# Two chunks per scan, scaled q and k in place, and a state gain every second chunk, in a fused HGRN2 and feed-forward kernel

## The chip, the cores and the metric

The kernel runs on one core of one Trainium2 chip. The metric is device time in microseconds (us). Three runs of the kernel before gave 463.27, 461.01 and 459.28 us, so the median is 461.01 us. One further execution was profiled; its times are in the section on the profile.

## The reference

An attention-like recurrence (4 batches, 8 heads, 768 steps, head width 48) feeds a feed-forward block on 3072 tokens. All data are fp32 on the chip.

```python
f = 1.0 / (1.0 + np.exp(-f_logit))
for t in range(S):
    state = f[:, :, t, :, None] * state + np.einsum('bhd,bhe->bhde', k[:, :, t], v[:, :, t])
    y[:, :, t] = np.einsum('bhd,bhde->bhe', q[:, :, t], state)
x = np.ascontiguousarray(attn_out.transpose(0, 2, 1, 3)).reshape(B * S, H * D)
a = x @ w1                      # w1, w2: 384 x 1024
b = x @ w2
h = a * b @ w3                  # w3: 1024 x 1024
return (h @ w_out)              # w_out: 1024 x 384
```

## The kernel before, in words

**Attention.** The 4 x 768 steps are 24 chunks of 128 steps (`C = 128`, `NU = 24`, six chunks per batch). A chunk's tile has the 8 heads as 2 groups of 48 partitions (padded to 112) and 4 heads of 128 steps side by side, so 512 columns (`NQ`). For each chunk `u`, `front(u)` plans: three pairs of loads (f, k, q, 96 KB each) and one of v; the sigmoid on ScalarE (`gates`, L521); a running product forward over the chunk (`forward`, a scan on VectorE, L529, into tile `fwd`); a copy of its last column (L534); the reciprocal of the last column into tile `back` (`ends`, L539); q times the product (`scale_q`, L545); a running product backward that starts from that reciprocal (`backward`, a scan, L551, into tile `bwd`); k times that (`scale_k`, L559). The scan's other operand (`floor` or `back`) starts the product anew at each head. With q and k scaled so, the chunk's own attention is a masked product of the two.

TensorE then turns k (`turn`, L598, 4 transposes; ScalarE copies the result into `kt`, L731). Every chunk from 4 on is handled by a **visit** (in `rest`), 13 rows of TensorE instructions that are always issued as one block: half of `values(u)` (L658), all of `pairs(u + 1)` (L584, the products of scaled q and k of the next chunk), the other half of `values(u)`, `from_state(u)` (L677), `update(u + 1)` (L690). After it ScalarE copies the outcome out of PSUM (`outcome`, L849, tile `ys`) and copies the products of the next chunk (tile `A`, L707); GpSimd masks them in two halves (`affine_select`, L713); VectorE forms the state in the middle and at the end of the next chunk (`middle`, L763 and L766). The state is carried on with a factor per row: GpSimd multiplies the last product with the next chunk's first gate (`gains`, L813, tile `G`), VectorE multiplies the state by it (L822). The next visit needs the mask, the middle state, the next chunk's q, k and `kt`, and the outcome copied. The outcome goes to DRAM and comes back turned (L870, then the gather `xt<-yt`, L873).

**Feed-forward.** Six blocks of 512 tokens. Weights come in as 8-byte words and are rounded by ScalarE (L1407) and VectorE (L1422, L1426, L1432); w3 and w_out are multiplied into one matrix (`fold`, L1471). Block 0 is plain products (`part`, L902 with 128x256), blocks 1 and half of 2 use seven products for eight (`seven`, L998), the others a larger scheme (`many`, L1153, its sums of weights on VectorE). The last product of each block is `down` (L902 with 128x192). Four PSUM banks (`f0` to `f3`) serve all these products and the transposes; four more (`l4` to `l7`) come free after the last visit.

**What sets the order.** Nothing is issued in program order: `Plan` holds every piece of work with its engine, a cost written in the code, what it depends on, which buffers it takes and a priority, and lists them by the earliest start and then by priority. Each engine's instructions are then issued in that order; the SyncE queue (SP) issues all DMAs in its order. Where the plan leaves TensorE idle early on, products of the constant tile `floor` are issued as filler, one for each 0.43 us:

```python
        if t["eng"] == "PE" and t["at"] < FULL:
            n = int((t["at"] - ready_at) / 0.43)
            if ready_at and n:
                idle(n)
            ready_at = t["end"]
```

Of the kernel before, what the change touches and what calls it, by code (L numbers as in the profile page):

```python
# [36 lines left out]
F32 = mybir.dt.float32  # L37
# [22 lines left out]
NQ = HP * C  # L60
NPE = 2
# [36 lines left out]
NFRONT = 12  # L98
# [28 lines left out]
FLOOR = 2.0**-60  # L127
RANGE = 2.0**-40
# [167 lines left out]
def ranged(ctx, tc, q, k, f_logit, v, w1, w2, w3, w_out, out, ident, w12, wc, left):  # L296
# [21 lines left out]
    gates_ = [keep.tile([P, NQ + 1], F32, name=f"gate{i}") for i in range(2)]  # L318
    inputs = [[keep.tile([P, NQ], F32, name=f"{nm}{i}") for i in range(n)] for nm, n in (("q", 3), ("k", 2), ("f", 2))]
    gate = [t[0:R] for t in gates_]  # L320
    qs, ks, fs = ([t[0:R] for t in ts] for ts in inputs)
# [7 lines left out]
    lasts = keep.tile([R, NU, HP], F32, name="lasts")  # L329
# [23 lines left out]
    early = abp.tile([P, KH, TB], F32, name="ab")[0:R]  # L353
    ks += [early[:, 0], early[:, 1]]
    fs += [early[:, 2], early[:, 3]]
    qs.append(at(12288, NQ)[0:R])
    dns = {nm: at(12288 + DH * i, DH) for i, nm in enumerate(("m1", "u2", "u3"))}

    homes = [lambda t=t: t[:, 0:NQ] for t in [floors] + gates_ + inputs[0] + inputs[1] + inputs[2]]
    homes += [lambda p=p, nm=nm: p.tile([P, NQ], F32, name=nm) for p, nm, n in ((one, "fwd", 1), (one, "bwd", 1), (work, "K", 2), (work3, "Q", 3), (work3, "ys", 3)) for _ in range(n)]  # L360
# [16 lines left out]
    plan.pools["t"][0:4] = [aside] * 4  # L377
    moving = plan.add("PE", 0.0, lambda: None, takes=["ab"], prio=-1e9)
    coming = plan.add("PE", 0.0, lambda: None, takes=["ab"], prio=-1e9)
# [29 lines left out]
    def setup():  # L409
# [3 lines left out]
        for i in range(2):  # L413
            if i == 0:
                nc.gpsimd.memset(ks[i][32:64], 0.0)
                nc.gpsimd.memset(qs[i][32:64], 0.0)
                make_identity(nc, ident)
            else:
                nc.gpsimd.memset(fs[i][32:64], 30.0)
        nc.gpsimd.memset(early[32:64, 2:4], 30.0)  # L420
        nc.gpsimd.memset(early[32:64, 0:2], 0.0)
        nc.gpsimd.memset(qs[2][32:64], 0.0)
        nc.gpsimd.memset(qs[3][32:64], 0.0)
        nc.vector.memset(floor, FLOOR)
        nc.vector.memset(heads(floor)[:, :, 0], 1.0)
        nc.vector.memset(back, 0.0)
        for t in gate:
            nc.vector.memset(t[:, NQ : NQ + 1], 0.0)
        nc.vector.memset(ks[1][32:64], 0.0)
        nc.vector.memset(qs[1][32:64], 0.0)  # L430
        for t in sb:
            nc.vector.memset(t, 0.0)

# [46 lines left out]
    def front(u):  # L480
# [3 lines left out]
        ask = n0 - 30 if u in (0, 1) or u > 3 else turn_of(str(u))  # L484
        ask = [ask, ask + 0.5, ask + 1.0, n0 - (28.2, 28.2, 28.2, 28.2, 12)[min(u, 4)] if u in (0, 1) or u > 3 else ask + VLATE[u - 2] if u in (2, 3) else ask + 1.2]

        def load(dst, src):
            def emit():
                if dst is fs[0] and u == 0:

                    nc.sync.dma_start(dst[0:64], src[u].rearrange("two d n -> (two d) n")[0:64])
# [6 lines left out]
        fu, qu, ku = (x[u if u < 4 else u % n] for x, n in ((fs, 2), (qs, 3), (ks, 2)))  # L498

        def free(n, *names):  # L500

            if u < 4:
                return []
            return asked[8:9] + [tk[u - n if u - n >= 4 else u % n][nm] for nm in names]

# [1513 lines left out]
```

## Time and profile before

| what | value |
|---|---|
| median of 3 runs | 461.01 us (459.28 to 463.27) |
| the profiled execution, whole time | 458.04 us |
| its span, first to last instruction | 456.2 us |
| TensorE busy in the span | 448.7 us, 98% |
| VectorE busy | 371.1 us, 81% |
| ScalarE, GpSimd busy | 212.0 us (46%), 69.1 us (15%) |
| granted TensorE clock | 1.00 |

The whole time is 1.8 us longer than the span. PE is TensorE's matmul, PEld its weight load, DVE VectorE, ACT ScalarE, POOL GpSimd, SP the queue that issues DMAs. In a timeline row the first number is the start in us from the start of the span, the second the duration; a fp32 product gives two records of a matmul.

### The profile page before, as it was taken

How to read it: one execution, taken by the hardware profiler on the slowest of the kernel's cores; microseconds unless marked ns; L12 is line 12 of the kernel's file. 1: busy time of each engine (PE TensorE's matmuls, PEld its weight loads, DVE VectorE, ACT ScalarE, POOL GpSimd, SP SyncE). 2: the span in 40 equal slices, each digit the busy share in tenths (PEclk: the TensorE clock that was granted, in tenths of full speed). 3: DMA queues.
4: the chain of work that ended last, by engine and by line, in shares of the span. 5: the costliest groups of instructions: out<-in, count | busy, mean ns of one | idle time of the engine just before them, and what ended most of it. 6: DMA issues, size and time to landing. Idle time of an engine off the chain costs nothing.

```text
span 456.2 us, 11781 instructions
## 1 busy us (share of the span) xinstructions
PE 448.7 (98%) x4792; PEld 392.5 (86%) x4792; DVE 371.1 (81%) x651; ACT 212.0 (46%) x473; POOL 69.1 (15%) x90
## 2 busy tenths in 40 slices
PE   7999999999999999999999999999999999999996
PEld 6788886666899888889999888899899988889996
DVE  8997899999898999989999699885659466767641
ACT  4565344432234453443323256665665666675300
POOL 9341000131222531223223000000000000000000
PEclk9999999999999999999999999999999999999999
DMA  6897898833236666356323502446365612233111
GB/s 178 268 339 249 300 340 284 271 108 105 71 100 196 180 175 162 105 155 184 97 73 82 147 16 78 138 141 205 132 194 172 204 60 96 91 93 92 37 69 39
DMA packets 43308, 68.74 MB, mean 151 GB/s; under 512 B 5217, under 2 KB 28386, under 8 KB 42226
## 3 DMA queue, kind: packets, MB, share of 16 engines
q1 hardware_dynamic: 43250, 67.95, 48.6%
q8 instruction: 38, 0.62, 0.6%
q14 instruction: 20, 0.16, 0.1%
HBM read 58.88 MB, written 9.04 MB: 149 GB/s over the span
## 4 chain that ended last, share of the span: by engine, by line
PE 95%; DVE 1%; SPq 1%; DMA 1%; POOL 0%; issue 0%; POOLq 0%; DVEq 0%
PE f L902 25%; PE l L1153 15%; PE f L998 13%; PE f L1153 12%; PE f L1471 9%; PE l L902 9%; PE py L658 3%; PE pa L584 2%; PE f L598 2%; PE py L677 2%; PE pa L690 2%; PE f L402 1%; SPq L495 1%; DMA ab<-in_k_dram 1%; DVE K L559 0%
## 5 line engine op out<-in xcount | busy, mean ns | idle before, releaser
L713 POOL TENSOR_SCALAR_AFFINE_SELECT A<-A 64x512 f32<-64x512 f32 (+1 forms) x46 | 46.2, 1004 | 107.8 <-ACT A L707 105.7
L1471 PE MATMUL f<-place 128*128 128x384 f32 x128 | 42.4, 487 | 0.0
L902 PE MATMUL f<-xt,w 128*128 128x256 f32 x192 | 42.1, 380 | 0.0
L902 PEld LDWEIGHTS f<-xt,w 128*128 128x128 f32 x192 | 36.3, 190 | 5.0
L1471 PEld LDWEIGHTS f<-place 128*128 128x128 f32 x128 | 23.9, 190 | 15.5
L902 PE MATMUL f<-place 128*128 128x192 f32 x176 | 31.9, 327 | 0.0
L998 PE MATMUL f<-xt,w 128*128 128x256 f32 x120 | 31.3, 380 | 0.0
L551 DVE TENSOR_TENSOR_SCAN bwd<-gate,back 112x512 f32<-112x512 f32 x24 | 30.4, 1267 | 0.7
L529 DVE TENSOR_TENSOR_SCAN fwd<-gate,floor 112x512 f32<-112x512 f32 x24 | 30.0, 1251 | 1.2 <-ACT gate L521 0.3
L902 PEld LDWEIGHTS f<-place 128*128 128x128 f32 x176 | 28.9, 190 | 0.4 <-issue 0.2
L849 ACT ACTIVATE ys<-py 112x512 f32<-112x512 f32 x22 | 13.1, 597 | 32.4 <-PE py L677 29.9
L1407 ACT ACTIVATE place<-place 128x512 f32<-128x512 uint32 (+2 forms) x24 | 21.4, 890 | 9.7 <-DMA place<-in_w_dram 8.7
L998 PEld LDWEIGHTS f<-xt,w 128*128 128x128 f32 x120 | 22.5, 190 | 2.9
L902 PE MATMUL f<-wc,ab 128*128 128x192 f32 x128 | 23.6, 328 | 0.0
L813 POOL TENSOR_TENSOR G<-lasts,gate 112x4 f32<-112x4 f32 x20 | 12.3, 614 | 72.3 <-ACT lasts L534 28.7
L902 PEld LDWEIGHTS f<-wc,ab 128*128 128x128 f32 x128 | 21.2, 190 | 0.3
L521 ACT ACTIVATE gate<-f 112x512 f32<-112x512 f32 x22 | 13.9, 631 | 16.4 <-DVE bwd L551 7.2
L902 PE MATMUL l<-place 128*128 128x192 f32 x112 | 19.8, 326 | 0.0
L658 PEld LDWEIGHTS py<-A,vt 64*64 64x64 f32 (+1 forms) x672 | 13.3, 127 | 7.3 <-issue 6.3
L998 PE MATMUL f<-place 128*128 128x256 f32 x72 | 19.1, 386 | 0.0
L902 PEld LDWEIGHTS l<-place 128*128 128x128 f32 x112 | 18.5, 190 | 0.1
L658 PE MATMUL py<-A,vt 64*64 64x64 f32 (+1 forms) x672 | 18.0, 223 | 0.2
(288 smaller groups left out, 1063.4 us busy)
## 6 DMA issues: line engine op xcount, KB each, us to landing
place<-in_w_dram SPq DMA_DIRECT2D x21, 512.0 KB, 5.9
A<-in_w_dram SPq DMA_DIRECT2D x19, 512.0 KB, 4.0
place<-in_w_dram SPq DMA_DIRECT2D x8, 1024.0 KB, 6.3
q<-in_q_dram SPq DMA_DIRECT2D x46, 96.0 KB, 2.9
vt<-in_v_dram SPq DMA_DIRECT2D x23, 192.0 KB, 2.9
out_dram<-o SPq DMA_DIRECT2D x23, 192.0 KB, 2.8
k<-in_k_dram SPq DMA_DIRECT2D x44, 96.0 KB, 2.4
yt<-ys SPq DMA_DIRECT2D x44, 96.0 KB, 2.9
```

The costliest lines, as they stand in the source:

```text
L521: nc.scalar.activation(gate[u % 2][:, 0:NQ], fu, AF.Sigmoid)
L529: nc.vector.tensor_tensor_scan(s["P"], gate[u % 2][:, 0:NQ], floor, 0.0, ALU.mult, ALU.max)
L551: nc.vector.tensor_tensor_scan(s["R"][:, ::-1], gate[u % 2][:, NQ:0:-1], back[:, ::-1], 0.0, ALU.mult, ALU.max)
L658: done = nc.tensor.matmul(y_block(u, hp, par, half)[p0 : p0 + w], lhsT=s["v"][half * W : half * W + W, h * D : h * D + w], rhs=s["A"][half ...
L713: nc.gpsimd.affine_select(out=a, in_=a, pattern=pattern, compare_op=ALU.is_ge, fill=0.0, base=0, channel_multiplier=-1,)
L813: nc.gpsimd.tensor_tensor(s["G"], lasts[:, u], heads(gate[(u + 1) % 2][:, 0:NQ])[:, :, 0], ALU.mult)
L849: nc.scalar.activation(ys, py, AF.Copy, accum_out=ysum[:, u : u + 1])
L902: nc.tensor.matmul(out_, lhsT=lhs[i], rhs=rhs[i], start=start and i == 0, stop=i == len(lhs) - 1, skip_group_check=True,)
L998: nc.tensor.matmul(q[nm][:, which * TH : which * TH + TH], lhsT=lhs[i](which), rhs=rhs[i], start=start and which == 0 and i == 0, stop=i = ...
L1153: nc.tensor.matmul(banks[g, c][:, which * TH : which * TH + TH], lhsT=lhs, rhs=x_node(a), start=first and which == 0, stop=True, skip_grou ...
L1407: nc.scalar.activation(part_.bitcast(F32), part_, AF.Copy, bias=2.0, scale=2.0**-51)
L1471: nc.tensor.matmul(w3s["p", jc], lhsT=w3s[jc][:, kc * P : kc * P + P], rhs=wos[:, kc], start=(kc == 0), stop=(kc == KF - 1),)
```

## The change

Chunks 0 to 3 (`ALONE = 4`) keep their own `front`. From chunk 4 on, `front_of_two(e)` serves chunks e and e + 1 together: loads of 192 KB for both, one sigmoid over 1024 columns, one forward scan and one backward scan over 1024 columns with 256 steps for a head, one product each for q and k. The backward scan writes into the gate's tile and the products into the tiles of q and k, so the tiles `fwd`, `bwd`, `K` and `Q` go. The two chunks share one running product, so the even chunk's state needs no gain: `gains` and `state` are planned for the odd chunk alone. A small memset after each backward scan takes the reciprocals out of `back` again, since `back` now serves as the other operand of the forward scan too. The floor of the running product (2^-60) is gone with it, and the limit under which the general path is taken is 2^-80 instead of 2^-40. A visit is planned as two pieces of work, `in` (half the values, then `pairs(u + 1)`) and `v` (the rest): what waits for the pairs, such as the copy of `A` and the mask, now follows `in`.

```diff
+N2 = 2 * NQ
+ALONE = 4
-NFRONT = 12
-FLOOR = 2.0**-60
-RANGE = 2.0**-40
+RANGE = 2.0**-80
...
-    floors = keep.tile([P, NQ], F32, name="floor")
+    floors = keep.tile([P, 2 * C], F32, name="floor")
-    spare = keep.tile([P, NQ], F32, name="back")
+    spare = keep.tile([P, N2], F32, name="back")
+    gates_ = [keep.tile([P, N2 + 2], F32, name=f"gate{i}") for i in range(2)]
+    raw_f = keep.tile([P, N2], F32, name="f")
+    running = keep.tile([P, N2], F32, name="run")
+    inputs = [[keep.tile([P, N2], F32, name=f"{nm}{i}") for i in range(2)] for nm in "qk"]
...
+        nc.vector.memset(floor, SMALL)
+        nc.vector.memset(back[:, 0:NQ], 0.0)
+        nc.vector.memset(heads(back[:, 0:NQ])[:, :, 0], 1.0)
...
+        nc.vector.memset(back[:, NQ:N2], 0.0)
+        nc.vector.memset(back[:, NQ : N2 : 2 * C], 1.0)
...
+    def front_of_two(e):
...
+        def load(dst, src):
+            def emit():
+                for par in range(2):
+                    to = dst[rows(par)].rearrange("p (k n) -> p k n", k=2)
+                    nc.sync.dma_start(to, src[e : e + 2, par].rearrange("k d n -> d k n"))
+            return emit
...
+        one_, two_ = of((e - 4, e - 3), "a", "t"), of((e - 4, e - 3), "v")
+        t["lf"] = moves(2, 394, 300, load(raw_f, f_logit), asked[8:9] + of((e - 2, e - 1), "g"), ask[0], since=since)
+        t["lk"] = moves(2, 394, 300, load(ku, k), asked[8:9] + one_, ask[1], since=since)
+        t["lq"] = moves(2, 394, 300, load(qu, q), asked[8:9] + one_ + two_, ask[2], since=since)
...
+        def gates():
+            nc.scalar.activation(by_run(gate[0:R, 0:N2]), by_head(raw_f), AF.Sigmoid)
+        def forward():
+            nc.vector.tensor_tensor_scan(P_, gate[0:R, 0:N2], back, 0.0, ALU.mult, ALU.max)
+        def scale_q():
+            to = by_head(qu)
+            nc.vector.tensor_tensor(to, to, by_run(P_), ALU.mult)
+        def backward():
+            nc.vector.tensor_tensor_scan(R_[:, ::-1], R_[:, ::-1], back[:, ::-1], 0.0, ALU.mult, ALU.max)
+            nc.vector.memset(heads2(back)[:, :, 2 * C - 1], 0.0)
+        def scale_k():
+            to = by_head(ku)
+            nc.vector.tensor_tensor(to, to, by_run(R_), ALU.mult)
...
-            def visit():
+            def enter():
                 s["py"] = ps.tile([P, 2, NQ], F32, name="py")
                 values(u, 1)
                 if more:
                     pairs(u + 1)
+
+            def visit():
                 values(u, 0)
                 from_state(u)
                 if more:
                     update(u + 1)
-            t["v"] = plan.add(
-                "PE", 0.15 + 0.46 * (2 - 0.5 * opens + 2 * more), visit,
+            t["in"] = plan.add(
+                "PE", 0.15 + 0.46 * (0.5 + more), enter,
                 [t["c"], t["lv"], t["mid"]] + past(u, 1, "y", *([] if opens else ["d"])) + [after[nm] for nm in ("q", "k", "e", "lv") if after],
                 n0 - 998, slack=0.8,
             )
+            t["v"] = plan.add("PE", 0.46 * (1.5 - 0.5 * opens + more), visit, [t["in"]], -1e7)
             if after:
-                after["a"] = after["s"] = t["v"]
+                after["a"], after["s"] = t["in"], t["v"]
...
-        if not closes:
+        if not closes and u >= ALONE and u % 2 == 0:
+            t["d"] = t["mid"]
+        elif not closes:
             def gains():
```

The sums of weights that `many` keeps in dead attention tiles now wait for finer groups of them (`k_old`, `q_old`, `k_new` beside `fronts`).

What the plan makes of it is read from the order of the built kernels. TensorE's matmuls are the same in number and shape, but for the fillers: 24 before, 25 after. A visit's 13 rows still stand together everywhere. Three places matter.

The first is SP's queue around chunk 3's gather (`xt<-yt_585` before, `xt<-yt_575` after), the last one that block 0 waits for. Before:

```order
L870 DMA yt_585<-ys_576 48x4x128 x2
L495 DMA f0_102<-in_f_logit_dram 48x512 x2
L495 DMA k0_100<-in_k_dram 48x512 x2
L495 DMA q1_98<-in_q_dram 48x512 x2
L873 DMA xt_311<-yt_585 128x3x128
L1403 DMA place_111<-in_w_out_dram 128x2x768 x3
L1403 DMA place_111<-in_w3_dram 128x2048
```

After:

```order
L970 DMA yt_575<-ys_566 48x4x128 x2
L588 DMA f_97<-in_f_logit_dram 48x2x512 x2
L588 DMA k0_101<-in_k_dram 48x2x512 x2
L588 DMA q0_99<-in_q_dram 48x2x512 x2
L973 DMA xt_303<-yt_575 128x3x128
L1503 DMA place_110<-in_w_out_dram 128x2x768 x3
L1503 DMA place_110<-in_w3_dram 128x2048
```

The order is the same; the six loads ahead of the gather now bring two chunks and have twice the bytes.

The second is TensorE where the first product of `down` follows the last plain product of block 0. Before (the fillers are L402):

```order
L902 MATMUL f3_1259<-xt_311,w12_59 128x256 x3
L902 MATMUL f0_1271<-xt_311,w12_59 128x256 x3
L902 MATMUL f1_1277<-xt_311,w12_59 128x256 x3
L402 MATMUL f3_1289<-floor_93 128x256 x2
L902 MATMUL f2_1292<-wc_60,ab_522 128x192 x4
L902 MATMUL f3_1299<-place_111 128x192 x4
```

After (the fillers are L412; the rows L768 and L781 end the visit of chunk 7):

```order
L768 MATMUL py_1241<-q1_100,S_1098 48x64 x8
L768 MATMUL py_1241<-q1_100,A_103 48x64 x8
L781 MATMUL pa_201<-vt_1100,kt_1225 48x48 x16
L412 MATMUL f3_1321<-floor_93 128x256 x3
L1002 MATMUL f1_1325<-wc_60,ab_512 128x192 x4
L1002 MATMUL f3_1335<-place_110 128x192 x4
```

The visit of chunk 7 has moved ahead of that place, and three fillers stand there instead of two. One more filler stands alone after the twelfth product of block 0, where none stood, and of two in the start-up one has gone.

The third is ScalarE's order after visits, where `A` is the copy that the mask waits for and `ys` the outcome. Before:

```order
L849 ACTIVATE ys_1547,ysum_108<-py_1468 112x2x2x128
L707 COPY A_104<-pa_203 128x512
L1289 COPY o_1564<-f0_1458 128x192
L521 ACTIVATE gate0_95<-f0_102 112x512
L731 COPY kt_1588<-f2_1574 128x448
L534 COPY lasts_107<-fwd_1602 112x4
```

After:

```order
L798 COPY A_103<-pa_201 128x512
L949 ACTIVATE ys_2258,ysum_107<-py_2183 112x2x2x128
L614 ACTIVATE gate1_96<-f_97 112x1024
L1142 COPY ab_2281<-f0_2129 128x256
L822 COPY kt_2283<-f2_2271 128x448
L798 COPY A_103<-pa_201 128x512
L949 ACTIVATE ys_2353,ysum_107<-py_2285 112x2x2x128
```

The copy of `A` now stands ahead of the outcome of the same visit, and the sigmoid over two chunks can stand between two visits. On TensorE two sets of four transposes now often stand side by side, and from chunk 11 on the visits have less between them: between the visits of chunks 15 and 16 there are four products of 256 columns and eight transposes, between those of 16 and 17 six such products. The first two products of `many` in block 2 now come beside the visits, from chunk 15's on, in bank f3, and the third product of that bank comes only after the last visit.

More of the change, by code (lines that the diff above doesn't have):

```diff
@@ L549, in backward @@
         def backward():
[L550 removed]
+            s["R"] = running[0:R, NQ:N2]
             nc.vector.tensor_tensor_scan(
[L552 removed]
+                s["R"][:, ::-1], gate_of(u)[:, NQ:0:-1], back[:, 0:NQ][:, ::-1], 0.0, ALU.mult, ALU.max
             )
[L555 removed]
+            nc.vector.memset(heads(back[:, 0:NQ])[:, :, C - 1], 0.0)
```

176 lines of the change are left out of this document (108 added, 68 removed).

## The prediction

> **What bounds the kernel now.** I read the page first: busy shares, then the chain of work that ended last.
>
> ```profile
> span 456.2 us, 11781 instructions
> PE 448.7 (98%) x4792; PEld 392.5 (86%) x4792; DVE 371.1 (81%) x651; ACT 212.0 (46%) x473; POOL 69.1 (15%) x90
> PE 95%; DVE 1%; SPq 1%; DMA 1%; POOL 0%; issue 0%; POOLq 0%; DVEq 0%
> ```
>
> TensorE is busy 98% of the span and carries 95% of the chain. An average hides stages, so I cut the span by stage; the columns are the window, its length, busy time and records of PE, PEld, DVE, ACT and POOL, then the granted clock, the DMA share and GB/s. Below them stand the same cuts for the fillers alone (L402: PE, PEld).
>
> ```profile
> 0.00:26.00 26.00, 23.03 (x246) 19.11 (x247) 22.69 (x36) 13.82 (x28) 16.66 (x31) 1.00 0.79 242
> 26.00:60.00 34.00, 33.80 (x332) 29.20 (x331) 29.97 (x35) 16.27 (x33) 5.02 (x5) 1.00 0.86 290
> 60.00:130.00 70.00, 70.00 (x664) 49.67 (x663) 65.70 (x90) 25.03 (x48) 11.18 (x12) 1.00 0.59 185
> 130.00:360.00 230.00, 229.90 (x3075) 209.44 (x3074) 196.11 (x374) 112.07 (x264) 36.22 (x44) 1.00 0.48 139
> 360.00:440.00 80.00, 80.00 (x411) 73.39 (x410) 51.67 (x106) 44.21 (x99) 0.00 (x0) 1.00 0.27 86
> ```
>
> ```profile
> 0.00:26.00 26.00, 10.73 (x38) 8.29 (x39) 1.00 0.79 242
> 26.00:60.00 34.00, 1.93 (x8) 1.04 (x6) 1.00 0.86 290
> 60.00:130.00 70.00, 1.03 (x4) 0.76 (x4) 1.00 0.59 185
> ```
>
> From 26 us on TensorE has no hole to speak of: 33.80 of 34, 70 of 70, 229.90 of 230, 80 of 80, all at clock 1.00. Fillers hide some waits: 1.93 + 1.03 = 2.96 us of them stand behind 26 us. So all that any relief of another engine could win after 26 us is 2.96 + 0.20 + 0.10 = 3.3 us. Before 26 us there are 10.73 us of fillers and 26.00 - 23.03 = 2.97 us of idle TensorE, and there VectorE (22.69 of 26) and the loads (0.79) set the pace.
>
> **The change, part by part.** All sums are against the profiled execution: span 456.2, whole time 458.04. The median of the runs, 461.01, is 2.97 above it; I add that at the end.
>
> *VectorE's relief.* Groups of VectorE, with busy time, mean ns of one, and idle before:
>
> ```profile
> L529 DVE TENSOR_TENSOR_SCAN fwd<-gate,floor 112x512 f32<-112x512 f32 x24 | 30.0, 1251 | 1.2 <-ACT gate L521 0.3
> L551 DVE TENSOR_TENSOR_SCAN bwd<-gate,back 112x512 f32<-112x512 f32 x24 | 30.4, 1267 | 0.7
> L559 DVE TENSOR_TENSOR K<-k,bwd 112x512 f32<-112x512 f32 x22 | 16.9, 770 | 0.4
> L545 DVE TENSOR_TENSOR Q<-q,fwd 112x512 f32<-112x512 f32 x23 | 16.2, 704 | 0.0
> 113.45 0.68 DVE L1504 TENSOR_TENSOR place<-w 128x512 f32<-128x512 f32 x1
> 118.57 0.95 DVE L1518 TENSOR_TENSOR place<-wc 128x768 f32<-128x768 f32 x1
> ```
>
> No row shows 1024 columns. 256 more columns of a plain product cost 0.95 - 0.68 = 0.27, so 512 more cost 0.54 and a product of 1024 takes 0.68 + 0.54 = 1.22. A scan of 1024 lies between 1.25 + 0.54 = 1.79 and 2 x 1.25 = 2.50. I take 2.36: the product's part that does not grow is 0.68 - 0.54 = 0.14, and a scan that saves just that gives 2.50 - 0.14. Per pair of chunks before: 4 x 1.26 + 2 x (0.770 + 0.704) = 7.99; after: 2 x 2.36 + 2 x 1.22 + 0.07 for the memset (my guess from 0.06 for the smallest one below) = 7.23. Ten pairs save some 8 us of VectorE, with a little more for reciprocals and gains left out. None of it reaches the end: the 3.3 us above is the cap, whatever VectorE saves. The same goes for ScalarE (46%), GpSimd (15%) and the fewer loads. Were this cover gone, VectorE's 8 us would be the most to lose or win.
>
> The single `f` tile makes the next pair's load wait for this pair's sigmoid. Two visits, some 10 us, lie between two such sigmoids and a load lands in about 3 us (the next fence but one): nothing. The backward scan now overwrites the gate, so it waits for GpSimd's gain of the chunk before; the forward scan ahead of it (2.36) covers that unless both masks stand in front. Behind it on VectorE are k's product and the middle states, which a visit waits for; I put this wait into the term on visits.
>
> *Start-up.* Here VectorE does bind. In these rows the first figure is the start, the second the duration:
>
> ```profile
> 1.07 0.48 DVE L424 MEMSET floor<- 112x512 f32 x1 [1.07 <-PEq L2006]
> 1.62 0.06 DVE L425 MEMSET floor<- 112x4 f32 x1
> 4.73 1.23 DVE L529 TENSOR_TENSOR_SCAN fwd<-gate,floor 112x512 f32<-112x512 f32 x1 [0.26 <-ACT gate L521]
> 23.92 0.96 DVE L1422 TENSOR_SCALAR place<-place 128x1536 uint32<-128x1536 uint32 x1 [0.30 <-DMA place<-in_w_dram]
> 28.02 1.76 DVE L1432 CUSTOM_DVE_ANT_0 w<-place,w 128x3072 uint16<-128x3072 uint16 x1
> 30.11 4.05 PE L902 MATMUL f<-xt,w 128*128 128x256 f32 x18
> ```
>
> The memsets ahead of the first scan change by: half of `floor` less (-0.24), the second half of `back` more (+0.48), two more gate columns and one more row of ones (3 x 0.06), so +0.42. The scan waited 0.26 for the gate, so it starts 0.16 later. Four memsets behind the backward scans of chunks 0 to 3 add 4 x 0.07 = 0.28. Of these 0.44, the wait of 0.30 for a load at 23.92 swallows up to 0.30. What is left goes through the weights' rounding (28.02) to the first block-0 product at 30.11: **+0.2**, between 0 and 0.5.
>
> *Chunk 3's gather.* Six loads ahead of it have twice the bytes now.
>
> ```profile
> 35.47 32.64 PE L902 MATMUL f<-xt,w 128*128 128x256 f32 x150
> 36.00:48.00 12.00, 12.00 (x57) 10.57 (x56) 9.64 (x10) 5.13 (x12) 1.20 (x1) 1.00 0.80 259
> 42.39 0.39 SPq L873 DMA_DIRECT2D xt<-yt  x1
> DMA to landing us min/median/max: 2.7/3.4/4.1
> ```
>
> The gather is issued at 42.39 and lands within 2.7 to 4.1 us (tile xt), by 46.5 at the latest. A record of these products takes 32.64 / 150 = 0.2176. By the order nine products of six records go ahead of the first that needs chunk 3: 35.47 + 54 x 0.2176 = 47.2, so 0.7 is spare. 576 KB more at 259 GB/s take 2.2 us, which would make the gather 1.5 late if all of it goes first; with the DMA share at 0.80, part finds room. A filler of 0.43 stands there now, so the cost is at least that unless TensorE comes late anyway. I take **+0.45**, between 0.43 and 1.5; 3.0 if the issues double in time as well.
>
> *Three fillers ahead of `down`.*
>
> ```profile
> 123.12 1.03 PE L402 MATMUL f<-floor 112*128 112x256 f32 x4
> 123.39 0.42 DVE L944 TENSOR_TENSOR ab<-f,ab 128x256 f32<-128x256 f32 x1 [0.83 <-PE f L902]
> ```
>
> Two fillers ran 1.03 while VectorE formed `ab` until 123.81: the wait that they cover was real, about 0.7 us. After, a visit's products stand ahead of three fillers; if the wait is gone, the third is pure loss. **+0.45**, one filler; from -0.3 (they start that much sooner on the free engine) to 1.5, where VectorE comes to `ab` a scan late.
>
> *Visits closer together.* One visit before, with the copies, masks and scans behind it:
>
> ```profile
> 152.94 0.45 PE L658 MATMUL py<-A,vt 64*64 64x64 f32 x16
> 153.21 0.64 PE L584 MATMUL pa<-Q,K 48*64 48x64 f32 x32
> 154.62 0.60 ACT L849 ACTIVATE ys<-py 112x512 f32<-112x512 f32 x1 [0.61 <-PE py L677]
> 154.82 1.99 PE L998 MATMUL f<-place 128*128 128x256 f32 x8
> 155.20 0.58 ACT L707 COPY A<-pa 128x512 f32<-128x512 f32 x1
> 155.64 1.23 DVE L529 TENSOR_TENSOR_SCAN fwd<-gate,floor 112x512 f32<-112x512 f32 x1
> 155.85 3.06 POOL L713 TENSOR_SCALAR_AFFINE_SELECT A<-A 64x512 f32<-64x512 f32 x2 [2.57 <-ACT A L707]
> 156.65 0.55 PE L598 MATMUL f<-ident,K 112*128 112x112 f32 x4
> 157.24 1.23 DVE L551 TENSOR_TENSOR_SCAN bwd<-gate,back 112x512 f32<-112x512 f32 x1
> 159.73 0.45 PE L658 MATMUL py<-A,vt 64*64 64x64 f32 x16
> 169.18 1.37 POOL L713 TENSOR_SCALAR_AFFINE_SELECT A<-A 64x512 f32<-64x512 f32 x2 [3.20 <-ACT A L707]
> ```
>
> The visit took 154.82 - 152.94 = 1.88; the next came 6.79 after its start. The masks ended at 158.91, 5.97 after the start, so 0.82 was spare. After, `A` is copied ahead of `ys`. The pairs end at 153.85, so the copy can start about 1.27 sooner, near 153.93: the masks would end 4.70 after the start if they are slow (3.06), 3.0 if they are quick (1.37, as at 169.18). Against that the distance shrinks. By the order shown, chunk 16's visit follows chunk 15's after four products (two records each, 4 x 0.435) and eight transposes (two times 0.55 at most, by the row at 156.65): 1.88 + 1.74 + 1.1 = 4.7 at most. The next comes after six products: 1.88 + 2.61 = 4.5. I count ten visits from chunk 11 on with about 4.5 to 5.5. Quick masks leave 1.4 spare, slow ones nothing, and the sigmoid over two chunks (about twice 0.6) can stand ahead of a copy of `A`. I take **+1.0**, a tenth of a us for each of the ten; from 0 to the 7 us of the first rival.
>
> **Sum.** 0.2 + 0.45 + 0.45 + 1.0 = +2.1: 460.1 for an execution like the profiled one, 463.1 on the scale of the median; I say 463.0.
>
> **Rivals.**
>
> *Slower: the scans of two chunks lock GpSimd out.* The masks at 155.85 took 3.06 beside the scans at 155.64 and 157.24, and 1.37 at 169.18. A mask that waits out a scan waits up to 2.36 - 1.23 = 1.13 longer now, two masks 2.26: 4.70 + 2.26 = 6.96 after the visit's start against a distance of 4.5 to 4.7, so TensorE stands still for some 2.4 us. Five scan pairs fall into the ten close visits. Three such hits are 7.2 in place of the 1.0: 466.3, on the median's scale 469.3. From two hits on (+3.8 on my forecast) it is slower by more than 1%. Against it: a mask that meets a plain product or nothing does not pay, and `A` comes sooner.
> The Trainium skill's page "SBUF — State Buffer", section "Who interferes with whom", says that a VectorE instruction with two SBUF inputs contends with a GpSimd instruction that reads SBUF, through an exclusive lock that holds the other off for its whole length. By that rule each half mask could wait for a whole scan of two chunks; the 3.06 beside two scans agrees with it.
>
> *Bank f3 held.* The first two products of `many` keep bank f3 from chunk 15's visit past the last one, which leaves three banks. Seven sevens or downs in that stretch that each wait for one eviction (0.42 at 123.39, up to 0.7 with the signals) cost 3 to 5 us: 463 to 465, median's scale 466 to 468. Against it: TensorE found a bank all the time before, with evictions by two engines.
>
> *No change.* The fillers cover waits that exist anyway and the closer visits find their masks ready: +0, 458.0, or 461.0.
>
> *Faster.* It would need the 3.3 us cap (457.7, which is still within 1%) and a shorter start-up, though every edit there adds work to VectorE. No row speaks for it.
>
> **How the numbers follow.** 1% is 4.6 us, about what a measurement of this kernel can tell; the runs shown lie 1.7 under and 2.3 over their median. My forecast has 0.54 (0.02 of it above 1%), no change 0.20, GpSimd locked out 0.13, bank f3 0.08 (0.05 above 1%), faster 0.05. That gives faster 0.05, same 0.20 + 0.52 + 0.03 = 0.75, slower 0.02 + 0.13 + 0.05 = 0.20. The range is 459.0 to 468.0: no change less the runs' scatter, up to bank f3's upper price; it leaves out most of GpSimd's 0.13 and the faster case.
>
> **What would show it.** VectorE's busy time falls by about 8 us with scans of 2.36 and products of 1.22, and TensorE's stays near 449. The first block-0 product starts near 30.3; the lone filler behind the twelfth product of block 0 runs without idle before the next; three fillers of 1.3 in all end later than `ab`. Right on the visits: TensorE idles about 1 us between 130 and 360, released by GpSimd's masks. Wrong: masks over 4 us with the next visit waiting 2 us or more (first rival); idle released by evictions of f0 to f2 (second); or a first block-0 product ahead of 30.1, which no step here allows.

## The result, and the profile after

The changed kernel took 473.96 us (median of 4 runs, 473.41 to 476.80) against 460.14 us (4 runs): a ratio of 1.0313, 95% interval 1.0265 to 1.0361. It is slower by 3.1%, and my range (459.0 to 468.0) failed by 6 us. The profiled execution took 473.41 us with a span of 471.6, 15.4 more than before. Its page, for the rows shown of before, and the row of the queue that brings TensorE's instructions:

```profile
span 471.6 us, 11599 instructions
PE 455.0 (96%) x4794; PEld 395.5 (84%) x4794; DVE 364.5 (77%) x610; ACT 208.5 (44%) x453; POOL 61.7 (13%) x80
q8 instruction: 39, 0.64, 0.7%
PE 76%; DVE 10%; issue 5%; DMA 3%; POOL 3%; SPq 1%; ACT 1%; DVEq 0%; POOLq 0%; ACTq 0%
```

VectorE does less (371.1 to 364.5) and TensorE ends later. "issue", time in which an engine waits for nothing that the profile shows, was 0% of the chain and is 5%. The stages as cut before, then the two pieces of 130 to 250 us of the change that matter, then those of before:

```profile
26.00:60.00 34.00, 32.73 (x325) 27.92 (x324) 28.13 (x31) 16.22 (x33) 3.17 (x4) 1.00 0.88 272
60.00:130.00 70.00, 70.00 (x776) 49.18 (x776) 66.20 (x79) 27.29 (x47) 13.27 (x11) 1.00 0.70 199
130.00:360.00 230.00, 222.59 (x2893) 200.16 (x2893) 179.00 (x313) 99.88 (x232) 31.10 (x36) 0.99 0.47 130
155.00:185.00 30.00, 25.73 (x682) 21.82 (x682) 22.20 (x33) 10.10 (x25) 8.01 (x9) 0.94 0.76 180
185.00:250.00 65.00, 63.24 (x1276) 55.70 (x1278) 56.26 (x87) 24.54 (x57) 16.76 (x20) 1.00 0.43 107
```

```profile
155.00:185.00 30.00, 30.00 (x607) 26.14 (x608) 28.10 (x50) 14.90 (x36) 11.13 (x14) 1.00 0.62 168
185.00:250.00 65.00, 65.00 (x1248) 59.10 (x1248) 60.66 (x107) 23.69 (x59) 17.07 (x22) 1.00 0.42 114
```

TensorE now has holes of 7.4 us between 130 and 360, 4.3 of them from 155 to 185, where its clock fell to 0.94. What it waited for (us in all, times, longest):

```profile
PE pa L781 <- issue: 3.8, 3, 2.1
...
PE py L749 <- POOL A L804: 1.3, 2, 1.0
...
PE f L1098 <- issue: 1.1, 1, 1.1
PE f L1002 <- DVE place L1369: 0.9, 2, 0.5
...
PE f L412 <- ACT ys L949: 0.8, 1, 0.8
PE f L1002 <- DMA xt<-yt: 0.4, 1, 0.4
```

The largest, 3.8 + 1.1 us, have no releaser. Here they stand in the timeline (start, duration, idle before), and two windows with the clock in the third figure from the end:

```profile
169.79 0.59 PE L1098 MATMUL f<-place,w 128*128 128x256 f32 x2
170.22 0.59 PE L1098 MATMUL f<-xt,w 128*128 128x256 f32 x2
171.90 0.59 PE L1098 MATMUL f<-place,w 128*128 128x256 f32 x2 [1.08 <-issue]
...
174.27 0.53 PE L781 MATMUL pa<-vt,kt 64*48 64x48 f32 x27
176.89 0.29 PE L781 MATMUL pa<-vt,kt 64*48 64x48 f32 x5 [2.09 <-issue]
...
184.32 0.42 PE L781 MATMUL pa<-vt,kt 64*48 64x48 f32 x17 [1.02 <-issue]
```

```profile
178.00:180.00 2.00, 2.00 (x8) 1.63 (x7) 1.93 (x5) 1.11 (x4) 1.50 (x2) 0.62 1.08 221
180.00:182.00 2.00, 2.00 (x36) 1.26 (x38) 1.11 (x3) 0.00 (x0) 0.00 (x0) 0.53 1.06 223
```

TensorE stops in the middle of an update (27 records, a pause of 2.1 us, 5 more), where no engine and no load releases it. The trace also holds each packet of queue q8: 39 of them, 16,384 bytes each, for TensorE's 4794 matmul, 4794 weight-load and 90 other records (waits and branches), so 248 records to a packet on average. Counting TensorE's records from 0 in order of time, the last record before every one of these stops is number 256 k + 192, and so it is before a stop of 0.7 us that ends at 30.26 us (k = 2). So I take a packet for a block of 256 instructions, and call a block entered when its first record starts. The block that follows a stop had just been fetched:

```
kernel   k   block k-1    fetch of        last record    block k      after the
             entered at   block k         before a stop  entered at   fetch's end
before  16   163.80       165.26-166.30     -            168.49       2.2
before  17   168.49       168.99-170.07     -            174.53       4.5
after   16   165.86       169.28-170.32   170.44         171.90       1.58
after   17   171.90       173.99-175.53   174.60         176.89       1.36
after   18   176.89       181.74-182.84   183.09         184.32       1.48
```

I read this as TensorE running out of instructions: the fetch began 2.1 to 4.9 us after the block before it had been entered (0.5 to 1.5 before), and what it brought was used 1.4 to 1.6 us after it ended. A visit (but for the first and the fifth of a batch) is exactly 256 records (128 matmuls, 128 weight loads) in 1.89 us; the close visits of the change start 4.6 to 5.8 us apart where nothing stops (6.3 or more before), so a block is used up sooner than a late fetch brings the next. The trace speaks for both being needed: at 198 to 207 and 239 to 248 us the visits start 4.6 to 4.7 us apart, the closest of all, the fetches begin 0.7 to 1.4 us after the block before is entered, and no block is missing.

For the account I give each TensorE product its mean start-to-start time in the kernel before and leave fillers out. Equal sums of this work cut each kernel into the same five stretches, named by the times at which the kernel before reaches them; the table shows by how much the profiled execution of each kernel took longer for a stretch, up to its last product. It is good to some 0.3 us.

```
us longer than before      0-60   60-155  155-185  185-250  250-end   sum
the change                 +2.6     +1.3     +6.8     +3.9     +0.4  +15.1
place in blocks moved     +13.2     +2.0     +1.4     +3.7     +0.4  +20.8
no loads of v              +2.7     +1.3     +1.9     +3.9     +0.4  +10.3
visits spaced              +3.9     +2.8     +0.1     +0.0     +0.0   +6.8
visit planned as one       +2.6     +5.6     +0.1     +1.8     +0.3  +10.4
no late fillers            +0.1     +1.4     +2.0     +4.0     +0.4   +7.9
gather ahead               +0.9     -0.1     +5.6     +6.7     +0.4  +13.5
early copy of A            +1.6     +2.9     +6.0     +5.3     +0.6  +16.5
masks of one column        +2.2     +1.3     +6.3     +3.2     +0.4  +13.4
no late fillers, spaced    +0.2     +1.2     -0.2     +2.4     +0.0   +3.7
before, visit in two       +0.6     +0.9     +0.1     +5.0     +0.8   +7.2
before, more loads         +0.9     +0.9     +3.8     +1.4     +0.0   +7.0
```

### The profile page after: what moved, and what is told of

Same layout as the page of the kernel before. It is cut to its first block, busy times and chain, and to the rows that moved or that the text cites. A ratio compares the mean times of both kernels' runs of the same rounds, so it can differ in the third digit from the quotient of the medians.

```text
span 471.6 us, 11599 instructions
## 1 busy us (share of the span) xinstructions
PE 455.0 (96%) x4794; PEld 395.5 (84%) x4794; DVE 364.5 (77%) x610; ACT 208.5 (44%) x453; POOL 61.7 (13%) x80
## 4 chain that ended last, share of the span: by engine, by line
PE 76%; DVE 10%; issue 5%; DMA 3%; POOL 3%; SPq 1%; ACT 1%; DVEq 0%; POOLq 0%; ACTq 0%
PE f L1002 17%; PE f L1253 15%; PE l L1253 10%; PE l L1002 9%; PE f L1098 9%; PE f L1571 4%; PE py L749 2%; POOL A L804 2%; PE l L1098 2%; PE pa L675 2%; PE py L768 1%; PE f L689 1%; DMA yt<-ys 1%; PE pa L781 1%; DVE place L1604 1%
## 5 line engine op out<-in xcount | busy, mean ns | idle before, releaser
L1002 PE MATMUL f<-xt,w 128*128 128x256 f32 x192 | 42.6, 380 | 0.4 <-DMA xt<-yt 0.4
L1002 PEld LDWEIGHTS f<-xt,w 128*128 128x128 f32 x192 | 36.2, 190 | 5.8 <-issue 0.7
L1571 PEld LDWEIGHTS f<-place 128*128 128x128 f32 x128 | 23.9, 190 | 15.4
L798 ACT COPY A<-pa 128x512 f32<-128x512 f32 x22 | 12.9, 587 | 48.3 <-PE pa L781 35.4
L1098 PE MATMUL f<-xt,w 128*128 128x256 f32 x100 | 27.5, 398 | 0.0
L642 DVE TENSOR_TENSOR_SCAN gate<-gate,back 112x1024 f32<-112x1024 f32 x10 | 23.9, 2394 | 0.7
L621 DVE TENSOR_TENSOR_SCAN run<-gate,back 112x1024 f32<-112x1024 f32 x10 | 23.1, 2307 | 0.1
L1098 PEld LDWEIGHTS f<-xt,w 128*128 128x128 f32 x100 | 19.5, 197 | 2.8
L1002 PE MATMUL l<-place 128*128 128x192 f32 x120 | 21.6, 326 | 0.0
L1002 PEld LDWEIGHTS l<-place 128*128 128x128 f32 x120 | 19.9, 190 | 0.1
L1647 ACT ACTIVATE A<-A,back 128x512 f32<-128x512 f32 x23 | 18.0, 782 | 0.2
L412 PE MATMUL f<-floor 112*128 112x256 f32 x50 | 15.7, 466 | 2.1 <-DVE floor L431 1.3
L1274 ACT COPY ys<-f 128x512 f32<-128x512 f32 x21 | 12.3, 586 | 10.6 <-PE f L1253 10.6
```

Source lines behind the costliest of these rows:

```text
L412: nc.tensor.matmul(to, lhsT=floor[:, 0:P], rhs=floor[:, 0:TH], start=True, stop=True)
L621: nc.vector.tensor_tensor_scan(P_, gate[0:R, 0:N2], back, 0.0, ALU.mult, ALU.max)
L642: nc.vector.tensor_tensor_scan(R_[:, ::-1], R_[:, ::-1], back[:, ::-1], 0.0, ALU.mult, ALU.max)
L798: nc.scalar.copy(s["A"].rearrange("p r h c -> p r (h c)"), s["pa"][:, :, 0 : HP * W])
L1002: nc.tensor.matmul(out_, lhsT=lhs[i], rhs=rhs[i], start=start and i == 0, stop=i == len(lhs) - 1, skip_group_check=True,)
L1098: nc.tensor.matmul(q[nm][:, which * TH : which * TH + TH], lhsT=lhs[i](which), rhs=rhs[i], start=start and which == 0 and i == 0, stop=i = ...
```

## The experiments

My theory after the result: F, TensorE's instruction blocks come late, since visits stand close and loads come in bursts. The rival M: masks or other engines that come late, the first rival of the prediction.

**The place in the blocks moved.**

```diff
-    plan.add("PE", 7.8, lambda: idle(9), prio=-1e8)
+    plan.add("PE", 7.8, lambda: idle(40, 64), prio=-1e8)
```

> The changed kernel with 40 fillers of 64 columns in place of the first 9 of 256, before TensorE has any data: 31 more products, four instructions each, so all that follows stands 124 places later in TensorE's stream of instructions; loads, visits and every other engine stay as they are. Theory F (TensorE runs out of instructions: its 16 KB blocks of 256 come late): the stops at 170.4, 174.6 and 183.1 us, which stand at places 256 k + 193 of the stream, move to other points of the visits or go; the place 256 k + 193 stays the place of every stop without a named releaser. The time moves by 2 us or more, most likely down to 466 to 471. Rival M (the stops are masks or other engines that come late): the same stops of 1.2, 2.3 and 1.2 us at the same products, 473 to 475.

479.27 us, ratio 1.046 (1.0435 to 1.0484). The total missed, for a cause of my own making: the 40 small fillers took 0.43 us each, 17.33 in all against 7.33, which is most of the +13.2 in the first stretch. Behind it loads, visits and order are the same, the stops are gone, and 155 to 185 takes 1.4 longer than before in place of 6.8. The waits for masks (1.3 us in all) stayed. This bears out F and speaks against M for these stops. With the ends of the blocks the fetches moved too: from 161 to 185 us they began 0.9 to 2.4 us after the block before was entered, so the run does not tell an end at a better place from a fetch that came sooner.

**Fewer data in the queues.**

```diff
+            if u >= 10:
+                st[u]["v"] = st[u - 3]["v"]
+                return
             st[u]["v"] = loads.tile([P, DM], F32, name="vt")
```

> The changed kernel without the loads of v from chunk 10 on (those chunks use an older v, 192 KB less per chunk to load); everything else issues in the same order. Theory F: the blocks of instructions wait behind less data, so the fetches that began 3.4, 2.1 and 4.9 us after the block before had been entered begin 1 to 2.5 us after it, the stops at 170 to 184 us shrink from 5.0 to under 2.5 us and the half clock behind them goes: 466 to 470. Rival M: no engine's work changes, 473 to 475. If the fetches come late for another reason than the data in the queues, their delays and the stops stay, too.

Chunks 10 to 23 use the v of an earlier chunk here, which leaves out loads and not products. 468.48 us, 1.0222 (1.0198 to 1.0247). The fetches of blocks 16 to 18 began 1.7, 1.0 and 2.9 us after the block before was entered (3.4, 2.1 and 4.9 with the loads); two stops of 0.4 and 1.0 us are left, the clock stays at 1.00, and 1.9 of the 6.8 remain. This fits F: with less data to load, the fetches began sooner.

**Visits spaced, and a visit planned as one.**

```diff
+            t["apart"] = plan.add("none", 4.2, lambda: None, [t["v"]])
```

> The changed kernel, but the plan lets at least 4.4 us pass between the end of a visit and the start of the next, so that 5.2 to 7 us of other products stand between visits from chunk 8 on, as before the change (4.3 to 8.7). Theory F: with 256 instructions spread over more time, each block arrives in time: the stops of 5.0 us and the half clock (about 1.7) go. Rival M: the waits for masks (1.9 us at 207 and 248 us) go and the stops at 170 to 184 stay. Both together: 473.4 - 6.7 - 1.9 = 465; only F: 467; only M: 471 to 472.

> The changed kernel with a visit planned as one piece, as before the change; loads, scans, products and memsets over two chunks stay. By its order 4.2 to 6.9 us of other products stand between most visits instead of 2.5 to 3.8. Theory F: most of the stops of 5.0 us and the half clock go, though the bursts of loads stay: 465 to 469. Rival: it is the loads of two chunks alone that make blocks late, and stops of 3 to 6 us stay at other places: 470 to 475.

Spaced: 464.89 us, 1.0134 (1.0098 to 1.017). Both kinds of wait are gone:

```profile
155.00:185.00 30.00, 30.00 (x595) 26.46 (x595) 25.07 (x39) 13.19 (x29) 8.00 (x9) 1.00 0.59 153
185.00:250.00 65.00, 65.00 (x1261) 58.88 (x1261) 56.71 (x90) 22.58 (x53) 15.19 (x19) 1.00 0.46 118
```

Loads, scans and memsets over two chunks are all there, and TensorE has no hole from 155 to 250: the loss of that stretch hangs on the distance of the visits. That the total met the 465 expected for both is partly luck: 10.7 us came back from 155 to 250, where 8.6 had been counted, and the new order lost 2.8 more than the change ahead of 155. The visit planned as one piece, all else of the change kept: 466.75 us, 1.0151 (1.0111 to 1.0191); in its profiled execution, the slowest of its four (468.88), 155 to 250 takes 1.9 longer in place of 10.7, while the new order loses 5.6 elsewhere (60 to 155, a wait of 1.9 for VectorE's rounded weights among it).

**No late fillers, and the gather ahead.**

```diff
-FULL = 130.0
+FULL = 20.0
...
-        since = n0 - AHEAD if 4 < e < 8 else 0.0
+        since = 42.0 if e == 4 else n0 - AHEAD if e < 8 else 0.0
```

> The changed kernel without the 11 fillers that the plan places after its 20th us (one at 22.3 us of the trace, four at 25.7, two at 30.8, one at 48.9, three at 128.6). My prediction's step: a filler that stands where no wait is costs 0.43 us; four of them (48.9 and 128.6) would give 1.7 us back. What the trace of the change suggests instead: the waits at 48.9 (a gather) and at 128.6 (VectorE's sums) are there without fillers, and only the filler at 22.3 costs, since it waits 0.78 us for its PSUM bank: 0.8 back before 60 us and nothing at 128. All behind it stands 44 places earlier in TensorE's stream, so theory F also moves the stops at 170 to 184 us: 468 to 474.

> The changed kernel with chunk 3's gather ahead of the six loads of chunks 4 and 5 on SP's queue (those are asked for later). If these loads make the gather late, the wait and the filler near 49 us go: 1.2 us back by 54 us of the trace. The plan shifts with it: from chunk 11 on, eight of the distances between visits hold only 2.5 to 2.9 us of other products, more than in the changed kernel (five). Theory F then expects stops of 4 to 9 us behind 130 us, at places 256 k + 193 of TensorE's stream, so 470 to 477 in all; the rival that only the bursts of loads decide has no reason for more than the 5.0 us of the changed kernel.

Without late fillers: 467.29 us, 1.0175 (1.0143 to 1.0206). The first stretch takes 0.1 longer in place of 2.6, more than I expected to get back: the change's loss there was the fillers', as these rows of the change show.

```profile
22.29 0.70 PE L412 MATMUL f<-floor 112*128 112x256 f32 x2 [0.78 <-ACT ys L949]
...
30.26 0.57 PE L781 MATMUL pa<-place,kt 64*48 64x48 f32 x30 [0.70 <-issue]
...
31.73 4.05 PE L1002 MATMUL f<-xt,w 128*128 128x256 f32 x18
...
48.85 0.60 PE L412 MATMUL f<-floor 112*128 112x256 f32 x2
49.82 10.38 PE L1002 MATMUL f<-xt,w 128*128 128x256 f32 x47 [0.37 <-DMA xt<-yt]
```

A filler writes a PSUM bank, and at 22.29 it waited 0.78 for ScalarE to empty that bank, with real work behind it; at 29.36 the next block of instructions was missing. At 128 us the fillers did cover a wait: without them TensorE stood 1.8 us for VectorE's sums. Everything stood 44 places earlier in the stream, and 155 to 185 lost 2.0 in place of 6.8: one stop of 1.4 us is left, again behind record 256 k + 192.

With the gather ahead: 471.75 us, 1.0276 (1.0236 to 1.0316). The first stretch loses 0.9 in place of 2.6, so the bytes ahead of the gather cost up to 1.7. But F expected stops of 4 to 9 us here, and behind 130 us there is one of 0.6; the visits, closer than ever, waited 6.2 us for masks instead. M has its case after all, in this kernel:

```profile
156.03 2.29 DVE L621 TENSOR_TENSOR_SCAN run<-gate,back 112x1024 f32<-112x1024 f32 x1
157.69 3.82 POOL L804 TENSOR_SCALAR_AFFINE_SELECT A<-A 64x512 f32<-64x512 f32 x2 [5.03 <-ACT A L798]
158.76 2.29 DVE L642 TENSOR_TENSOR_SCAN gate<-gate,back 112x1024 f32<-112x1024 f32 x1
161.56 0.38 PE L749 MATMUL py<-A,vt 64*64 64x64 f32 x11 [1.74 <-POOL A L804]
```

The first half of the mask ends 0.5 us behind the first scan, the second half 0.5 us behind the second. The fetches give a reason why the stops stayed away: those that this trace holds behind 140 us began 0.6 to 1.9 us after the block before was entered, so visits that start 4.3 to 5.0 us apart got their blocks in time. Why the same loads made the fetches late at 169 to 182 us in the change, and not here, was not followed.

**The two-part visit alone, in the kernel before.**

```diff
-            t["v"] = plan.add(
-                "PE", 0.15 + 0.46 * (2 - 0.5 * opens + 2 * more), visit,
+            t["in"] = plan.add(
+                "PE", 0.15 + 0.46 * (0.5 + more), enter,
...
+            t["v"] = plan.add("PE", 0.46 * (1.5 - 0.5 * opens + more), visit, [t["in"]], -1e7)
```

> The kernel before with the visits planned in two parts as in the change, and nothing else of it: loads, scans and products stay at one chunk. By its order five distances between visits from chunk 6 on hold 3.0 to 3.9 us of other products, where before none held less than 4.3. If close visits alone starve TensorE of instructions: stops of 1 to 4 us, 461 to 464. If it takes the bursts of the loads of two chunks as well: no stops, 458 to 460. If the earlier copy of A is a gain on its own: 456 to 458.

465.71 us, 1.0134 (1.0102 to 1.0166), above what I expected of either side. Nearly all of it is lost behind 185 us, in many waits for VectorE and ScalarE of up to 1.5 us; of missing instructions there are 0.3 us. So visits that start 5.0 to 5.9 us apart, with the loads of one chunk, did not starve TensorE by themselves. This part of the change costs 6 us by itself; why VectorE comes late there I have not followed further.

**The copy of A, as I had read the change.** In the change's trace the copy still waits for the update:

```profile
155.57 0.45 PE L749 MATMUL py<-A,vt 64*64 64x64 f32 x16
...
156.99 0.53 PE L781 MATMUL pa<-vt,kt 64*48 64x48 f32 x16
...
157.65 0.59 ACT L798 COPY A<-pa 128x512 f32<-128x512 f32 x1 [2.23 <-PE pa L781]
```

```diff
                 if more:
                     pairs(u + 1)
+                    taken_now(u + 1)
```

> The changed kernel, but the copy of A is issued right behind the next chunk's pairs, inside the visit, ahead of the update. In the changed kernel's trace the copy still waits for the update's last product (it starts about 2.1 us after the visit's start, not 1.0 as my prediction had it). If the masks' lateness costs 1.9 us (207 and 248 us), that comes back and the copies start 0.7 us sooner; the update then waits for the copy by 0.1 to 0.2 us a visit, up to 3 us in 19. Theory F: the stops at 170 to 184 us are not touched by it. So 471 to 475; 466 or less would say that the late copies, not the blocks of instructions, were behind the stops.

474.27 us, 1.0313 (1.0218 to 1.0408), as expected: waits for masks fall to 0.5, the update waits for the copy instead, and a stop of 2.5 us for instructions stays.

```profile
PE pa L781 <- issue: 2.9, 2, 2.5
PE pa L781 <- ACT A L886: 2.4, 10, 0.4
...
PE py L749 <- POOL A L806: 0.5, 1, 0.5
```

**Masks of one column; more loads in the kernel before.**

```diff
+                n = W if u < 10 else 1
-                select(... [[0, H], [1, W]])
+                select(...[:, :, 0:n], [[0, H], [1, n]])
```

```diff
             loaded(s["v"], u)
+            if 8 <= u < 20:
+                more_ = dram.tile([4, P, DM], F32, name="more")
+                for i in range(4):
+                    nc.sync.dma_start(more_[i], v[(u + i) % NU])
```

> The changed kernel with the masks of chunks 10 to 23 cut to their first column (the rest of these chunks' products stays unmasked); nothing else changes, the order included. By the account of the trace the 3.8 us lost between 185 and 250 us are in part waits for masks that scans of two chunks hold off (1.9 us at 207 and 248 us): those go, 2 us in all, 471 to 472.5. The stops at 170 to 184 us (7.3 us) stay if they are TensorE's missing instructions. If masks are behind the stops as well, 465 or less; if they cost nothing, 473 to 474.5.

> The kernel before with four more copies of 192 KB, DRAM to DRAM, behind each load of v of chunks 8 to 19; nobody reads them, and the order of all else stays. Each chunk then moves some 1.9 MB in place of 1.15. If a block of TensorE's instructions waits behind whatever data is queued, blocks come 2 to 6 us late, and stops without a named releaser appear at places 256 k + 193 of TensorE's stream though the visits stand as far apart as ever: 461 to 475, part of it waits for late loads, which the trace names. If it takes close visits as well, TensorE waits at most for late loads, and no such stops show.

Masks (from chunk 10 on the rest of these products stays unmasked): 471.05 us, 1.0255 (1.0217 to 1.0293). The stops for instructions stay (6.3 lost from 155 to 185), and only 0.7 of the 3.9 behind 185 us comes back, since even these masks were late: 0.52 us of work took 2.55 beside a scan.

```profile
199.71 0.52 POOL L804 TENSOR_SCALAR_AFFINE_SELECT A<-A 64x8 f32<-64x8 f32 x2 [6.78 <-ACT A L798]
204.23 2.55 POOL L804 TENSOR_SCALAR_AFFINE_SELECT A<-A 64x8 f32<-64x8 f32 x2 [4.00 <-ACT A L798]
...
204.47 2.28 DVE L621 TENSOR_TENSOR_SCAN run<-gate,back 112x1024 f32<-112x1024 f32 x1
```

More loads: 464.82 us, 1.0125 (1.0107 to 1.0142), but not by F. Behind 130 us the fetches began at most 2.5 us after the block before was entered, and at most 0.2 us was lost at the end of a block; TensorE waited instead for VectorE behind late loads (2.9 us for `K`; 2.0 for a state, which stood on VectorE behind sums that waited 4.5 us for a gather). Data in the queues alone did not starve it; with visits as far apart as before, a fetch had time.

**All repairs together.** The first has spaced visits, the gather ahead and no late fillers; the second no late fillers and visits spaced from chunk 10 on; the third adds the early copy to that; the fourth is the kernel before without late fillers.

> The changed kernel with visits at least 4.4 us apart, chunk 3's gather ahead of the loads, and no fillers after 20 us: all three repairs together, the attempt at a version that keeps the change and is not slower. From 464.9 with the spacing alone, 0.8 for the filler at 22 us and 1.9 for the gather (what it cost there) come off: 462, and 461 where the early stop of 0.6 us at 30 us moves too. Faster than before (458.9) would need a gain that no trace shows so far.

> The changed kernel without the fillers planned after 20 us, and with visits at least 4.4 us apart from chunk 10's on. If the account is whole, its parts add: without those fillers the kernel stood 1.4 us behind the kernel before at 155 us of the trace, and spaced visits lose from there on what the kernel before loses (4.1 against 3.7 by 250 us): 459.3 + 1.4 + 0.4 = 461, between 460 and 463. If something else of the change costs time as well (scans, loads, memsets over two chunks), it stays at 464 or more.

> As the run without late fillers and with spaced visits, and the copy of A right behind the pairs. If masks are no longer late at this distance, the copy gains nothing and costs the update's wait of 0.1 to 0.2 us in 19 visits: 461 to 465. If a late mask is still part of what is left, 459 to 461.

> The kernel before without the fillers planned after 20 us (its 2.96 us of fillers behind 26 us and two pieces before it). If fillers only cover waits: 458.5 to 460. If they cost time here as they do in the changed kernel (2.6 us by 60 us of the trace): 456.5 to 458. They could also be worth having, where TensorE's clock falls without them: 460 to 463.

The first: 462.42 us, 1.0058 (1.0029 to 1.0087), as expected, and no better than the kernel before. The second: 464.11 us, 1.01 (1.0061 to 1.0138), 1 to 4 us above my account; its profiled execution (461.93) loses 3.7, 2.4 of it from 185 to 250 us (a missing block of 0.7 among it). Its ten runs lie between 461.88 and 466.92, wider than those of the kernel before, and I can't say why. I had said that 464 or more would mean that scans, loads or memsets over two chunks cost time as well; the median stands at that mark and the profiled execution well under it, so this stays open. The third: 467.83 us, 1.0148 (1.0066 to 1.023), worse than expected: the update's waits of 2.4 us and a stop of 1.3 us for instructions. The fourth: 458.04 us, 0.9968 (0.9933 to 1.0003): the fillers of the kernel before cost nothing that can be told. No version with the change beats the kernel before.

## Why the prediction was wrong, step by step

**The bound** was read rightly: TensorE's cap of 3.3 us left VectorE nothing to give. VectorE's busy time fell by 6.6 us (I said about 8), and no kernel gained by it.

**The prices** held:

```profile
L642 DVE TENSOR_TENSOR_SCAN gate<-gate,back 112x1024 f32<-112x1024 f32 x10 | 23.9, 2394 | 0.7
L621 DVE TENSOR_TENSOR_SCAN run<-gate,back 112x1024 f32<-112x1024 f32 x10 | 23.1, 2307 | 0.1
L637 DVE TENSOR_TENSOR q<-q,run 112x1024 f32<-112x1024 f32 x10 | 12.6, 1264 | 4.3 <-DMA q<-in_q_dram 4.3
```

2.31 and 2.39 us for a scan (2.36 taken), 1.26 for a product (1.22).

**Start-up, +0.2:** the step that I worked out is right, since VectorE's chain is not later (its first rounding of weights started at 23.92 before):

```profile
23.70 0.96 DVE L1522 TENSOR_SCALAR place<-place 128x1536 uint32<-128x1536 uint32 x1
```

The first block-0 product still came 1.6 later (31.73 against 30.11), by a filler that waits for its bank and a missing block of instructions, neither of which I had as terms.

**Gather, +0.45:** the filler (0.43) and the wait of 0.37 behind it, at 48.85 and 49.82 above, are 0.8, and up to 1.7 by the run with the gather ahead, about the bounds of 0.43 to 1.5. **Three fillers, +0.45:** the whole stretch from 60 to 155 lost 1.3, but 1.4 without those fillers. The wait under them is VectorE's; it even outlasts them, by 0.54:

```profile
128.64 1.56 PE L412 MATMUL f<-floor 112*128 112x256 f32 x6
130.04 1.47 PE L1002 MATMUL f<-wc,ab 128*128 128x192 f32 x8
132.04 1.54 PE L1002 MATMUL f<-place 128*128 128x192 f32 x8 [0.54 <-DVE place L1369]
```

**Visits, +1.0: this step failed.** It measured 6.8 + 3.9 = 10.7 us. Two things were wrong in it. The copy of `A` was to start 1.27 us sooner: it starts 2.08 after the visit's start (157.65 - 155.57) in place of 2.26, since it still waits for the update, so the masks won next to nothing. And I priced closer visits by the masks alone. The wait that came was for instructions: moving the ends of the blocks gave 5.4 us of the 6.8 back, spacing the visits 6.7. The 6.8 hold the half clock of 178 to 182 us as well, some 1.7 us, which followed the stops; with the place moved, without the loads of v, with visits spaced and without late fillers the clock stays at 1.00 there.

**The rivals.** The first, GpSimd locked out (0.13), named a mechanism that the runs show, at its clearest in the kernel with the gather ahead (6.2 us). In the changed kernel its named waits are 1.3 us, not 7. I quoted the Trainium skill for it ("SBUF — State Buffer", "Who interferes with whom"); the one-column masks agree with that rule, 0.52 us of work held for 2.55. Bank f3 (0.08) is not seen: no wait for an eviction of f0 to f2 stands among those of the close visits. The rival that decided was not on the list. The Trainium skill has it, on "Runtime: NRT & Kernel Launch", section "Instruction fetch mechanics": instructions come in blocks of 256 by a queue of the engine's own while the one before is used up. The packets of 16,384 bytes agree. It calls the cost of a block's end mostly hidden; at most ends that holds here, but at three of them it was 1.0 to 2.1 us of idle, and the measurement decides.

**What stays open.** The 3.2 us that the stretch from 185 to 250 still loses with one-column masks, and the two-part visit's own 6 us, are many small waits for several engines. Spacing the visits takes the first away, so they come from closeness; which of them counts for how much was not settled. How much of a block's delay is queued data is shown only in part: taking away the loads of v took 1.1 to 1.9 us off each, while four more copies per chunk in the kernel before made no fetch later than 2.5 us.

## What to carry to other kernels

Where an engine's work is many short instructions, count them: a stretch that runs 256 instructions in under two microseconds needs the next block fetched within the pause that follows, so that pause is worth planning for like a bank or an engine. Before a change that moves such stretches together, set the distance between them against the time from one block's entry to the next block's use, which the packets of the instruction queue give. And read where a copy waits from the wait in the trace (the last writer of its tile), not from the order in which pieces are planned.

## What the runs showed of the hardware

- The stops of over 0.3 us that no engine and no load explains all stood behind record 256 k + 192 of TensorE's stream, in each kernel that had any, and TensorE went on 1.3 to 1.6 us after the fetch of the next block had ended. In the kernel before the closest calls left 1.29 and 1.45 us between a fetch's end and the block's first instruction, at 28.66 and 206.67 us: by that it was at the edge already.
- 40 products of 64 columns at the very start took 0.43 us each (17.33 us in all), as much as a product of 256 columns later (0.435).
- After stops of 1.1 and 2.1 us the granted clock fell to 0.62 and 0.53 from 178 to 182 us, in the middle of a kernel that otherwise kept 1.00. It is not instructions alone that do this: with the gather ahead it fell to 0.63 and 0.52 from 162 to 166 us, right behind a wait of 1.7 us for a mask. Nor does every such wait: with more loads in the kernel before it stayed at 1.00 behind a wait of 2.0 us.
- A mask of 8 elements a row, 0.52 us by itself for both halves, took 2.55 us beside one scan of two chunks and ended with it.
